# Gates of two more units from sums of logarithms, one unit's keys and queries turned on VectorE, and a load queue in written order

## The chip, the cores and the metric

The kernel runs on one core of a Trainium2 chip. That core has TensorE (PE, with its weight loads shown as PEld), VectorE (DVE), ScalarE (ACT), GpSimd (POOL), a queue engine (SP) that issues nearly all transfers here, and 16 DMA engines. The metric is device microseconds of one execution. The kernel before took 466.81 us in the median of four runs (466.21 to 467.61). A profile records one execution with the start and duration of each instruction; its times are us from the start of its span.

## The reference

There are two blocks, one after the other. The first is a gated linear attention over 4 batches, 8 heads, 768 steps and a head of 48:

```
f = 1 / (1 + exp(-f_logit))
for t in range(S):
    state = f[:, :, t, :, None] * state + k[:, :, t] (outer) v[:, :, t]
    y[:, :, t] = q[:, :, t] @ state
```

The second is a mixer on x, which is y with the heads side by side (768 x 384 per batch):

```
u   = x + ((x^T U) V)^T          # U: 768 x 32, V: 32 x 768
out = u + relu(u @ w_ch1) @ w_ch2   # w_ch1: 384 x 1536, w_ch2: 1536 x 384
```

Inputs are float32, but the four weights arrive as float64, and the kernel rounds them to float32 itself.

## The kernel before

**Units.** The recurrence is done two heads at a time. A unit n is a pair of heads of a batch, so there are 16 (NU); four (HP) make a batch. A unit's 768 steps stand in 12 chunks of 64. Inside a chunk the kernel needs, for each step, the product of the gates after it in the chunk (X, which scales the keys) and the product up to it (Y, in effect one over the first, which scales the queries). With these a chunk is ordinary products: scores of keys and queries (sc, L967), a mask (A, L980), the scores times v (inner, L1077), a turned copy of the keys (kept, L994), the chunk's addition to the state (ds, L1018), a scan over the chunks (L1043) and queries times states (y, L1059).

**Two ways to X and Y.** Units 0 to 3 go by logarithms: `logs` and `logs_end` take log(1 + exp(-f)) on the loaded tile (a floor on VectorE, Exp and Ln on ScalarE), `log_sums` (L820) makes the sums on TensorE by a product with a triangular matrix `later`, which turns the tile as well, and `keep_logs` (L832) takes exponentials of the sums on ScalarE. Units from 4 on go by gates: `gates` (L851) turns f and applies Sigmoid, `keep` (L866) runs a backward scan on VectorE for X with four small instructions after it, and `read` (L884) a forward scan for Y. The tiles `fz` hold the gates and need a zero at each chunk's start (L1269, L1270).

**Three ways to turn.** Channels have to lie in the partitions. For units 0 to 5 `load` (L630) brings the tensors in rows of 48 numbers and TensorE turns them, six 128x128 transposes a tensor (`on_tensor`, L777). Units 6 and later (TURNED is 6) are loaded in blocks of 32 steps in eight smaller transfers for two tensors (L661), and VectorE turns them in 32x32 blocks (`turned`, L754). `operand` (L786) turns keys or queries and multiplies them by X or Y.

**Weights.** 27 blocks of float64: one of U, two of V, twelve of w1, twelve of w2. A block is loaded into a ring of four buffers, halved on ScalarE (two instructions, L91 and L92), joined on VectorE (L98 to L100) and added on POOL (L101). `ahead_by` starts block i+11 when it joins block i; the load has to wait until the block four before it has left its buffer.

**The order around the change.** VectorE and ScalarE run in the order in which the code is written up to the second batch's mixer, TensorE throughout. SP's order is the written one up to `written.close()` (L1246), before mixer 0 starts; behind it a scheduler sets it. The mixer's first product for batch 0 (ch1, L300) then runs as 17 pieces of 12 matmuls, `m.firsts[1:]`, behind one piece that turns x. After each piece a weight block or two is joined, and from piece number EARLY on one step of the generator `second` is taken. `second` first brings the front of unit 4 and then `steps` (L1118) for units 4 to 8, with the fronts of 5 to 9 in between. A front is five pieces: gates, keep, keys, read, queries. `follow` (L768) loads the tensor of two units ahead when a tensor has been used. What is left of `second` after ch1 goes on in `attention`, where `Fill` spreads the pieces of ch2 (L355, three matmul pairs each) evenly over the remaining steps: a fixed number of portions sets the share of each step, and what is left over runs at the end. In before 35 steps and 35 portions remain. The stretch ends with the first product of the next mixer (ph, L184).

PSUM has three large buffers (`big`: transposes, scores, states, y) and two smaller ones (`mm`: ch1 and ch2), used in turn.

Of the kernel before, what the change touches and what calls it, by code (L numbers as in the profile page):

```python
# [14 lines left out]
AF = mybir.ActivationFunctionType  # L15
ALU = mybir.AluOpType
# [11 lines left out]
FLOOR = -40.0  # L28
# [128 lines left out]
class Mixer:  # L157
# [6 lines left out]
    def __init__(self, tc, b, x, U, V, w1, w2, sums, ident, blocks, out, two, three, zp, ps_big, ps_mm, wide=False,  # L164
                 z_all=None, room=None, pair=0):
        nc = tc.nc
# [8 lines left out]
        uT, z, h, S = {}, {}, {}, {}  # L175
# [161 lines left out]
        self.some = low_rank_of, added_up_of, mix_of, turn_of, ch1_of  # L337

        def store(t, o, cols=slice(0, DM)):
            n = 1 if b else 2  # L340
            for r in range(n):
                g = slice(r * P // n, (r + 1) * P // n)
                nc.sync.dma_start(out=out[b, t * P + g.start : t * P + g.stop, cols], in_=o[g, cols])
# [221 lines left out]
def factored_path(ctx, tc, q, k, v, f_logit, moe_U, moe_V, moe_w_ch1, moe_w_ch2, out, ok):  # L565
# [4 lines left out]
    nc = tc.nc  # L570
    B, H, S, D = q.shape
    P = nc.NUM_PARTITIONS
    C = P // 2
# [3 lines left out]
    HP = H // 2  # L577
# [11 lines left out]
    TURNED = HP + HP // 2  # L589
# [40 lines left out]
    def load(n, *names):  # L630

        b, hp = divmod(n, HP)
        for nm in names:
            if nm == "v":
                v_tiles[n] = three.tile([P, NBL, 2, D], F32, name="v_nat")
            for par in range(2):
                head = src[nm][b, 2 * hp + par]
                if nm in "kq" and n < HP:
                    if par == 0:
                        nc.sync.dma_start(  # L640
                            out=packed(n, nm).rearrange("p (h t) -> p h t", h=2),
                            in_=src[nm][b, 2 * hp : 2 * hp + 2].rearrange("h (p c) d -> p h (c d)", p=P),
                        )
                    continue
                if nm == "v" and par:

                    for s in range(2):
                        nc.sync.dma_start(
                            out=v_tiles[n][(1 - s) * C : (2 - s) * C, :, par, :],
                            in_=head.rearrange("(c s p) d -> s p c d", s=2, p=C)[s],  # L650
                        )
                    continue
                if nm == "v" or n < TURNED:
                    dst = v_tiles[n] if nm == "v" else nat[n % 2][nm]
                    nc.sync.dma_start(out=dst[:, :, par, 0:D], in_=head.rearrange("(c p) d -> p c d", p=P))
                    continue
                head = head.rearrange("(c i) d -> i c d", i=NB)
                for part in range(2):
                    p0 = par * PAD + part * NB
                    n_ch = min(NB, D - part * NB)  # L660
                    nc.sync.dma_start(  # L661
                        out=raw[n % 2][nm][p0 : p0 + NB, :].rearrange("p (c d) -> p c d", d=NB)[:, :, 0:n_ch],
                        in_=head[:, :, part * NB : part * NB + n_ch],
                    )
# [95 lines left out]
    def prepare(n):  # L760


        T = units[n] = {}
# [4 lines left out]
        def follow(nm):  # L768

            if n >= HP and n + 2 < NU:  # L770
                load(n + 2, nm)

        def on_tensor(nm):

            pt = ps_big.tile([P, 2, 512], F32, name="pt", tag="big")
            for c in range(NBL):
                nc.tensor.transpose(  # L777
                    pt[:, 2 * c // NBL, c % (NBL // 2) * P : (c % (NBL // 2) + 1) * P],
                    nat[n % 2][nm][:, c].rearrange("p h d -> p (h d)"), ident,
                )  # L780
            return pt[:, :, 0 : G * C].rearrange("p a (c t) -> p a c t", t=C)

        def halves(t):
            return t[:, 0:S].rearrange("p (a c t) -> p a c t", a=2, t=C)

        def operand(nm, of):  # L786
            t = T[nm] = kz[n % 2][:, C:] if nm == "k" else two.tile([P, S], F32, name="qT")
            if n < HP:
                pt = on_tensor(nm).rearrange("p a c t -> p a (c t)").rearrange("p a (c t) -> p t a c", c=NBL // 2)
                by_time = "p (t a c) -> p t a c"  # L790
                nc.vector.tensor_tensor(t.rearrange(by_time, a=2, c=NBL // 2), pt,
                                        T[of].rearrange(by_time, a=2, c=NBL // 2), ALU.mult)
            elif n < TURNED:
                nc.vector.tensor_tensor(halves(t), on_tensor(nm), halves(T[of]), ALU.mult)
            else:
                turned(t, r[nm])
                nc.vector.tensor_tensor(t, t, T[of], ALU.mult)

        def unpack(nm):
            nc.vector.tensor_copy(  # L800
                nat[n % 2][nm][:, :, :, 0:D], packed(n, nm).rearrange("p (h c d) -> p c h d", h=2, c=NBL),
            )
# [47 lines left out]

        def gates():  # L851
            f0 = T["f0"] = two.tile([P, NCH], F32, name="f0")
            if n < TURNED:
                pt = on_tensor("f")
                nc.scalar.activation(halves(f)[:, :, :, 1:C], pt[:, :, :, 1:C], AF.Sigmoid)
                nc.scalar.activation(f0.rearrange("p (a c) -> p a c", a=2), pt[:, :, :, 0], AF.Sigmoid)
                follow("f")
                return
            fT = late[:, 6, :]
            turned(fT, r["f"])  # L860
            follow("f")
            fv = fT.rearrange("p (c t) -> p c t", t=C)
            nc.scalar.activation(by_chunk[:, :, 1:C], fv[:, :, 1:C], AF.Sigmoid)  # L863
            nc.scalar.activation(f0, fv[:, :, 0], AF.Sigmoid)
# [23 lines left out]
        def queries():  # L888
            operand("q", "Y")
            follow("q")  # L890

        if n < HP:
            return [logs, keep_logs, keys, log_sums, queries, logs_end, lambda: unpack("k"), lambda: unpack("q")]
        return [gates, keep, keys, read, queries]

    x_tiles = {}
# [196 lines left out]
    def front(n, *names):  # L1093

        if n >= NU:
            return []
        if n not in ahead:
            names_of = ("gates", "keep", "keys", "read_back", "queries", "gates_end", "unpack_k", "unpack_q")
            ahead[n] = dict(zip(names_of, prepare(n)))
        return [ahead[n].pop(nm) for nm in names if nm in ahead[n]]  # L1100
# [9 lines left out]
    def joined(*groups):  # L1110

        groups = [g for g in groups if g]
        for _ in groups[1:]:
            yield lambda: None
        if groups:
            yield lambda: [f() for g in groups for f in g]

    def steps(first, last):  # L1118

        def behind(n):  # L1120

            return HP + 3 <= n < NU - 1

        for n in range(first, last):
            if n < NU:
                yield from joined(rear(n - 2, "inner"), rear(n - 1, "scores"), rear(n, "kept"))
            else:
                for piece in rear(n - 2, "inner") + rear(n - 1, "scores"):
                    yield lambda: None
                    yield piece  # L1130
            if behind(n):
                yield from front(n, "read_back", "queries")
            if n + 1 < NU and n + 1 not in v_tiles:
                load(n + 1, "v")
            yield from front(n + 1, "gates", "keep", "keys")
            yield from joined(rear(n - 1, "read"), rear(n, "states", "scan"))
            if not behind(n + 1):
                yield from front(n + 1, "read_back", "queries")
            if n + 1 == last:
                yield from rear(n - 1, "inner")  # L1140
                if n + 2 < NU:
                    load(n + 2, "v")
# [30 lines left out]
    with tc.manual_schedule(engines={nc.vector.engine, nc.scalar.engine}):  # L1173
# [66 lines left out]
        low_rank_of, added_up_of, mix_of, turn_of, ch1_of = m.some  # L1240
        for load_w in weights[early + FIRST : early + FIRST + 4]:
            load_w[0]()
        load(HP + 1, "f", "k")
        weights[early + FIRST + 4][0]()
        load(HP + 1, "q", "v")
        written.close()  # L1246
        loads[early]()
        low_rank_of(done)
        for piece in rear(n, "read"):
# [15 lines left out]
        m.before[4][1]()  # L1265
        ch1_of(0, 0, (0, 2), (1, 2))
        loads = loads[early + 3 :]
        for t in fz:
            nc.vector.memset(t[:, 0:S].rearrange("p (c t) -> p c t", t=C)[:, :, 0], 0.0)  # L1269
            nc.vector.memset(t[:, S : S + 1], 0.0)  # L1270

        start = m.before[5:]

        EARLY = 3
        second = chain(front(HP, "gates", "keep", "keys", "read_back", "queries"), steps(HP, 2 * HP + 1))
        for i, (_, piece) in enumerate(start + m.firsts[1:]):
            piece()
            for f in loads[: 2 if i in (0, 2) else 1]:
                loads.remove(f)
                f()  # L1280
            if i >= EARLY:
                next(second)()
        for f in loads:
            f()
        n = len(m.seconds) // (NBL // 2)
        todo, after = m.seconds[:-n], m.seconds[-n:]

# [397 lines left out]
```

## Time and profile before

| what | value |
|---|---|
| median of four runs | 466.81 us |
| the profiled execution's own time | 466.64 us |
| its span, first to last instruction | 464.9 us |
| granted TensorE clock | 0.999 |
| busy: TensorE, VectorE, ScalarE, POOL | 456.1, 352.6, 166.3, 54.4 us |
| ch1 of mixer 0 with units 4 and 5 beside it | 48.15 to 99.40 us |
| ch2 of mixer 0 with units 4 to 7 beside it | 99.40 to 149.48 us |

How to read the lines that follow: a timeline line has the start, the time from the first to the last of its instructions, the engine, the source line, the operation, output and inputs, shapes and count; in brackets stand the idle time of that engine before it and what ended it ("issue" means that the profile shows no cause). A line by stretches has the stretch, its length, then the busy time and count of PE, PEld, DVE, ACT and POOL, the granted clock, the mean share of the DMA engines and GB/s. A float32 matmul is issued as two instructions, a transpose as one. Matmuls overlap, so their spacing, not their duration, is what one costs.

### The profile page before, as it was taken

How to read it: one execution, taken by the hardware profiler on the slowest of the kernel's cores; microseconds unless marked ns; L12 is line 12 of the kernel's file. 1: busy time of each engine (PE TensorE's matmuls, PEld its weight loads, DVE VectorE, ACT ScalarE, POOL GpSimd, SP SyncE). 2: the span in 40 equal slices, each digit the busy share in tenths (PEclk: the TensorE clock that was granted, in tenths of full speed). 3: DMA queues.
4: the chain of work that ended last, by engine and by line, in shares of the span. 5: the costliest groups of instructions: out<-in, count | busy, mean ns of one | idle time of the engine just before them, and what ended most of it. 6: DMA issues, size and time to landing. Idle time of an engine off the chain costs nothing.

```text
span 464.9 us, 13023 instructions
## 1 busy us (share of the span) xinstructions
PE 456.1 (98%) x5639; PEld 395.2 (85%) x5639; DVE 352.6 (76%) x582; ACT 166.3 (36%) x319; POOL 54.4 (12%) x60
## 2 busy tenths in 40 slices
PE   8999999999999999999999999999999999999997
PEld 6886888876666578999898888889989999999996
DVE  5768788979999677676765559977797886858652
ACT  6775776563332143323322222431312311212200
POOL 2002445634112001010000000120000000000000
PEclk9999999999999999999999999999999999999999
DMA  9948997577778704504533030100000000000001
GB/s 194 198 123 208 218 215 184 144 127 106 123 103 123 113 18 53 78 1 89 76 52 76 12 61 4 27 4 21 18 1 1 35 1 19 17 1 35 1 36 39
DMA packets 148583, 34.35 MB, mean 74 GB/s; under 512 B 136934, under 2 KB 146982, under 8 KB 148518
## 3 DMA queue, kind: packets, MB, share of 16 engines
q1 hardware_dynamic: 147718, 33.29, 36.7%
q8 instruction: 46, 0.75, 0.7%
q10 hardware_dynamic: 800, 0.15, 0.2%
q14 instruction: 19, 0.16, 0.1%
HBM read 28.70 MB, written 4.72 MB: 72 GB/s over the span
## 4 chain that ended last, share of the span: by engine, by line
PE 76%; DVE 14%; issue 3%; ACT 3%; DMA 2%; SPq 2%; POOL 0%; DVEq 0%; ACTq 0%; POOLq 0%
PE pw L389 26%; PE pz L300 18%; PE pp L495 12%; PE po L355 5%; PE y L1059 2%; SPq L661 2%; PE pt L777 2%; PE y L1077 1%; PE ds L1018 1%; PE pt L827 1%; PE sc L967 1%; DVE late L868 1%; DVE late L886 1%; PE pt L994 1%; DVE late L921 1%
## 5 line engine op out<-in xcount | busy, mean ns | idle before, releaser
L300 PE MATMUL pz<-uT,w 128*128 128x256 f32 x492 | 111.5, 382 | 0.3 <-ACT uT L289 0.2
L300 PEld LDWEIGHTS pz<-uT,w 128*128 128x128 f32 x492 | 91.7, 190 | 12.9 <-ACT uT L289 0.6
L1047 POOL COPY st<-added 128x576 f32<-128x576 f32 x12 | 18.2, 1519 | 187.5 <-DVE added L1043 187.5
L389 PE MATMUL pw<-zw,w_raw 128*128 128x192 f32 x216 | 38.0, 329 | 0.0
L389 PE MATMUL pw<-w,z_all 128*128 128x192 f32 x216 | 37.3, 327 | 0.0
L101 POOL TENSOR_TENSOR w<-w_y,w_r 128x384 int32<-128x384 int32 x24 | 31.5, 1314 | 36.9 <-DVE w_y L100 20.7
L389 PEld LDWEIGHTS pw<-w,z_all 128*128 128x128 f32 x216 | 35.3, 190 | 0.5
L389 PEld LDWEIGHTS pw<-zw,w_raw 128*128 128x128 f32 x216 | 35.1, 190 | 0.6 <-DVE w_y L204 0.3
L335 ACT ACTIVATE z_all<-pz 128x512 f32<-128x512 f32 x33 | 19.6, 598 | 44.3 <-PE pz L300 43.9
L868 DVE TENSOR_TENSOR_SCAN late<-fz,late 128x768 f32<-128x768 f32 x12 | 21.1, 1755 | 9.4 <-ACT fz L863 9.3
L488 ACT ACTIVATE other<-other 128x512 f32<-128x512 f32 x18 | 11.3, 632 | 40.3 <-DVE other L204 40.3
L355 PE MATMUL po<-w,zw 128*128 128x384 f32 x72 | 25.1, 495 | 0.0
L355 PE MATMUL po<-w,z_all 128*128 128x384 f32 x72 | 24.7, 493 | 0.0
L886 DVE TENSOR_TENSOR_SCAN late<-fz,other 128x768 f32<-128x768 f32 x12 | 22.0, 1835 | 0.2
L980 DVE TENSOR_TENSOR A<-sc,causal 128x768 f32<-128x768 f32 x16 | 15.2, 952 | 8.7 <-PE sc L967 8.7
L355 PEld LDWEIGHTS po<-w,zw 128*128 128x128 f32 x72 | 13.2, 190 | 9.6 <-issue 0.8
L355 PEld LDWEIGHTS po<-w,z_all 128*128 128x128 f32 x72 | 13.3, 190 | 8.9 <-DVE o L204 0.6
L488 ACT ACTIVATE z_all<-z_all 128x512 f32<-128x512 f32 x12 | 7.6, 631 | 34.1 <-DVE z_all L204 34.1
L1026 ACT COPY added<-ds 48x576 f32<-48x576 f32 (+2 forms) x29 | 17.9, 620 | 5.1 <-PE ds L1018 4.7
L1059 PEld LDWEIGHTS y<-st,qT 48*64 48x64 f32 x704 | 13.6, 137 | 6.6 <-issue 4.3
L495 PE MATMUL pp<-v_nat,late 128*128 128x128 f32 x152 | 19.1, 275 | 0.0
L98 DVE TENSOR_SCALAR w_y<-w_y 128x384 f32<-128x384 f32 (+3 forms) x27 | 12.2, 451 | 8.8 <-ACT w_y L91 8.6
(226 smaller groups left out, 869.0 us busy)
## 6 DMA issues: line engine op xcount, KB each, us to landing
w_raw<-in_moe_w_ch_dram SPq DMA_DIRECT2D x18, 384.0 KB, 3.6
out_dram<-o SPq DMA_DIRECT2D x17, 192.0 KB, 1.9
v_nat<-in_v_dram SPq DMA_DIRECT2D x16, 144.0 KB, 3.6
v_nat<-in_v_dram SPq DMA_DIRECT2D x32, 72.0 KB, 3.5
zw<-in_moe_w_ch_dram SPq DMA_DIRECT2D x6, 384.0 KB, 5.0
out_dram<-o SPq DMA_DIRECT2D x14, 96.0 KB, 2.2
w<-in_k_dram SPq DMA_DIRECT2D x4, 288.0 KB, 4.0
w<-in_q_dram SPq DMA_DIRECT2D x4, 288.0 KB, 4.4
```

The source lines that it names most:

```text
L101: nc.gpsimd.tensor_tensor(dst.bitcast(I32), shaped(y.bitcast(I32)), shaped(r), ALU.add)
L300: nc.tensor.matmul(pm[:, i * 2 * P : (i + 1) * 2 * P], lhsT=w1[:, m, o : o + P], rhs=uT[a][:, m, :], start=(m == 0), stop=(m == NDC - 1))
L335: nc.scalar.activation(z[a, c][:, k : k + 2, :].rearrange("p i t -> p (i t)"), pm, AF.Relu)
L355: nc.tensor.matmul(pm, lhsT=z[a, i // NI][:, i % NI, s * P : (s + 1) * P], rhs=w2[:, i, :], start=(i == 0), stop=(i == NFC - 1))
L389: nc.tensor.matmul(W["pm"][:, n * HM : (n + 1) * HM], lhsT=lhs[:, i, :], rhs=rhs[:, i, :], start=(i == 0), stop=(i == NI - 1))
L488: nc.scalar.activation(dst, dst, AF.Relu, scale=float(SIGNS[n]))
L495: nc.tensor.matmul(pm[:, i, r * P : (r + 1) * P], lhsT=room["w"](wn)[:, r * P : (r + 1) * P], rhs=x_node(a, xn), start=((xn, wn) == of[0]) ...
L868: nc.vector.tensor_tensor_scan(backwards(X, S - 1, S), backwards(f, S, S), backwards(ends, S - 1, S), 0.0, ALU.mult, ALU.add,)
L886: nc.vector.tensor_tensor_scan(Y, f[:, 0:S], starts, 0.0, ALU.mult, ALU.add)
L1026: nc.scalar.copy(added[r, 1:].rearrange("p (e c s) -> p e c s", c=NBL, s=2)[:, e], ds[r, :, 0 : NBL * D].rearrange("p s (c e) -> p e c s", ...
L1047: nc.gpsimd.tensor_copy(st, states.rearrange(by_e, c=NCH))
L1059: nc.tensor.matmul(o(c % 2, par, c // 2), lhsT=T["q"][rows[par], chunk[c]], rhs=T["st"][rows[par], c, :], start=(c <= 2), stop=False, skip ...
```

## The change

1. `load`: units up to 4 come in rows for all tensors, unit 5 for f alone. Keys and queries of unit 5 come in blocks of 32 and VectorE turns them.
2. Units 4 and 5 get new pieces in place of gates, keep and read: `bound` (the floor on VectorE), `sums_kept` (sums on TensorE, the load of the next f, the exponentials on ScalarE) and `logs_whole` (Exp and Ln on ScalarE). Their scans, sigmoids and small VectorE instructions are gone. The table of Sigmoid is first loaded by unit 6. The zeros of `fz` are written by units 6 and 7.
3. Order: `bound` and `logs_whole` of unit 4 stand ahead of `second`, those of unit 5 are joined to keys and queries of unit 4. EARLY becomes 4. So 48 steps remain in `second` instead of 50, 34 are left after ch1, and `Fill` counts 36 portions.
4. SP keeps the written order to the end of ch1; the keys and queries of unit 5 are loaded behind pieces 0 and 2.
5. `store` writes the last four blocks of batch 0 in one transfer each instead of two.

```diff
         def store(t, o, cols=slice(0, DM)):
-            n = 1 if b else 2
+            n = 2 if b == 0 and t < 2 else 1
...
-                if nm == "v" or n < TURNED:
+                if nm == "v" or n <= HP or (nm == "f" and n < TURNED):
...
         def gates():
             f0 = T["f0"] = two.tile([P, NCH], F32, name="f0")
-            if n < TURNED:
-                pt = on_tensor("f")
-                nc.scalar.activation(halves(f)[:, :, :, 1:C], pt[:, :, :, 1:C], AF.Sigmoid)
-                nc.scalar.activation(f0.rearrange("p (a c) -> p a c", a=2), pt[:, :, :, 0], AF.Sigmoid)
-                follow("f")
-                return
+            if n < TURNED + 2:
+                nc.vector.memset(by_chunk[:, :, 0], 0.0)
+                nc.vector.memset(f[:, S : S + 1], 0.0)
...
+        def bound():
+            fn = nat[n % 2]["f"][:, :, :, 0:D]
+            nc.vector.tensor_single_scalar(fn, fn, FLOOR, ALU.max)
+
+        def logs_whole():
+            fn = nat[n % 2]["f"][:, :, :, 0:D]
+            nc.scalar.activation(fn, fn, AF.Exp, scale=-1.0)
+            logs_end()
+
+        def sums_kept():
+            log_sums()
+            follow("f")
+            keep_logs()
+
         if n < HP:
             return [logs, keep_logs, keys, log_sums, queries, logs_end, lambda: unpack("k"), lambda: unpack("q")]
+        if n < TURNED:
+            return [bound, sums_kept, keys, logs_whole, queries]
         return [gates, keep, keys, read, queries]
...
-        load(HP + 1, "f", "k")
+        load(HP + 1, "f")
         weights[early + FIRST + 4][0]()
-        load(HP + 1, "q", "v")
-        written.close()
+        load(HP + 1, "v")
...
-        for t in fz:
-            nc.vector.memset(t[:, 0:S].rearrange("p (c t) -> p c t", t=C)[:, :, 0], 0.0)
-            nc.vector.memset(t[:, S : S + 1], 0.0)
-
         start = m.before[5:]
 
-        EARLY = 3
-        second = chain(front(HP, "gates", "keep", "keys", "read_back", "queries"), steps(HP, 2 * HP + 1))
+        EARLY = 4
+        second = chain(front(HP, "keep"), joined(front(HP, "keys"), front(HP + 1, "gates")),
+                       joined(front(HP, "queries"), front(HP + 1, "read_back")), steps(HP, 2 * HP + 1))
+        bound, logs = front(HP, "gates", "read_back")
+        bound()
         for i, (_, piece) in enumerate(start + m.firsts[1:]):
             piece()
+            if i == 1:
+                logs()
+            elif i in (0, 2):
+                load(HP + 1, "k" if i == 0 else "q")
             for f in loads[: 2 if i in (0, 2) else 1]:
                 loads.remove(f)
                 f()
             if i >= EARLY:
                 next(second)()
         for f in loads:
             f()
+        written.close()
```

More of the change, by code (lines that the diff above doesn't have):

```diff
@@ L781, in on_tensor @@
             return pt[:, :, 0 : G * C].rearrange("p a (c t) -> p a c t", t=C)
-        def halves(t):
-            return t[:, 0:S].rearrange("p (a c t) -> p a c t", a=2, t=C)
         def operand(nm, of):
@@ L792, in operand @@
                                         T[of].rearrange(by_time, a=2, c=NBL // 2), ALU.mult)
-            elif n < TURNED:
-                nc.vector.tensor_tensor(halves(t), on_tensor(nm), halves(T[of]), ALU.mult)
+            elif n == HP:
+                nc.vector.tensor_tensor(
+                    *[u.rearrange("p (a c t) -> p a c t", a=2, t=C) if u is not None else on_tensor(nm) for u in (t, None, T[of])],
+                    ALU.mult,
+                )
             else:
```

## The prediction

> **What bounds the kernel now.** I read the page's first two parts first, then the table by stretches, then the timelines of TensorE and VectorE in the stretch that the diff touches. The page, its busy times (engine, busy us, share of the span):
>
> ```profile
> PE 456.1 (98%) x5639; PEld 395.2 (85%) x5639; DVE 352.6 (76%) x582; ACT 166.3 (36%) x319; POOL 54.4 (12%) x60
> ```
>
> TensorE is busy for 456.1 of 464.9 us, so all its idle time is 8.8 us; 3.4 lie after its last product. The granted clock is 0.999, so no time hides there. The table by stretches (length, busy us and counts of PE, PEld, DVE, ACT, POOL, clock, DMA share, GB/s), cut where the mixer's ch1 (L300) ends and ch2 (L355) begins:
>
> ```profile
> 48.15:99.40 51.25, 51.25 (x364) 44.59 (x361) 45.90 (x75) 34.48 (x67) 26.28 (x21) 1.00 0.81 186
> 99.40:150.59 51.19, 50.41 (x866) 32.06 (x864) 45.37 (x61) 18.15 (x35) 10.67 (x7) 1.00 0.78 113
> ```
>
> In the first stretch TensorE never stops: work taken from other engines there is worth nothing, only TensorE's own instructions count. In the second it stops a little, and VectorE is nearly as full. The stops, in TensorE's timeline (start, us, count, idle time before):
>
> ```profile
> 99.40 4.03 PE L355 MATMUL po<-w,z_all 128*128 128x384 f32 x12
> ...
> 104.73 4.41 PE L355 MATMUL po<-w,zw 128*128 128x384 f32 x12
> ...
> 116.69 0.76 PE L1018 MATMUL ds<-v_nat,kb 64*48 64x48 f32 x48 [0.57 <-issue]
> ...
> 123.00 0.59 PE L994 MATMUL pt<-ident,kz 64*128 64x64 f32 x12
> ...
> 134.88 0.59 PE L994 MATMUL pt<-ident,kz 64*128 64x64 f32 x12 [0.21 <-DVE kz L797]
> ```
>
> Twelve po products take 3.97 us where they run freely (99.40 to 103.36); at 104.73 they take 4.35 (to 109.08): 0.38 of waiting for the last w2 block, whose POOL sum ends at 108.18. At 116.69 ds of unit 6 needs the PSUM buffer that the mask A of unit 5 frees; y before it needs 0.71 us elsewhere (103.36 to 104.07), so this stop is 116.69 - 115.22 - 0.71 = 0.76. The third is 0.21. Together 1.35 us. VectorE's timeline shows who is late:
>
> ```profile
> 101.94 0.97 DVE L754 STREAM_TRANSPOSE late<-late 128x768 f32<-128x768 f32 x1
> ...
> 105.65 1.75 DVE L868 TENSOR_TENSOR_SCAN late<-fz,late 128x768 f32<-128x768 f32 x1
> ...
> 109.52 0.96 DVE L797 TENSOR_TENSOR kz<-kz,late 128x768 f32<-128x768 f32 x1
> ...
> 115.64 0.95 DVE L980 TENSOR_TENSOR A<-sc,causal 128x768 f32<-128x768 f32 x1
> 116.51 0.97 DVE L754 STREAM_TRANSPOSE late<-other 128x768 f32<-128x768 f32 x1
> 118.37 1.76 DVE L868 TENSOR_TENSOR_SCAN late<-fz,late 128x768 f32<-128x768 f32 x1 [0.90 <-ACT fz L863]
> ...
> 121.65 0.96 DVE L797 TENSOR_TENSOR kz<-kz,late 128x768 f32<-128x768 f32 x1
> ```
>
> kz of unit 6 starts at 109.52, of unit 7 at 121.65: one unit costs VectorE 12.13 us, with 0.90 of waiting for the sigmoid. Here VectorE sets the pace of the keys and TensorE can only follow.
>
> **The change, part by part: TensorE.** Out go the gates' transposes of units 4 and 5 and the keys' and queries' of unit 5: 4 x 6 (L777), each six 0.66 us (56.02 to 56.68), 2.62. In come the sums of logarithms, 2 x 12 instructions of 130 columns (L827). Their row is 12 in 1.53 us (26.41 to 27.94). From below: the L300 rows give 256 columns in 216 ns (24 in 5.18), by the column 110 ns for 130, 1.32 per unit. I take 1.54, the same line's own row: +3.08. Net +0.46, from below +0.02, all of it in the full first stretch.
>
> **VectorE, first stretch.** Out: per unit scan, copies and reciprocal 2.85 (63.37 to 66.22) and the second scan 1.67 (69.83 to 71.50), 9.0 for two. In: two bounds (0.45, row L808) and two turnings of unit 5 (0.97, row L754), 2.9. Some 6 us of relief, worth nothing: VectorE has 5.35 us of idle time there already and waits for the weights' ACT halves, which TensorE's pieces pace.
>
> **ScalarE, first stretch.** In: Exp and Ln (0.69 each, L810 and L817) and the kept exponentials (0.8, 0.8, 0.2, 0.2), 3.4 per unit; out two sigmoids of 0.76 and a table load of 1.28. That adds 4.0 us to 34.48 of 51.25: hidden by the rest of 16.8. If the cover failed, ch1's PSUM buffers would come free late; each has a 2.6 us piece between filling and need, and the longest delay that I add up (Exp and Ln, 1.4) is under it. Memsets (0.07 each) have cover.
>
> **Loads.** The SP queue keeps to its written order. Keys of unit 5 stand behind weight block 16, queries behind 19, f of unit 6 behind 23, k behind 25. A weight load waits for the block four before it; by the rows of before (block 19's space free at 76, f's at 84.4, k's at 90.9) f6 is issued by 87 and k6 by 94, landing 3 to 4 us later. They are needed at some 100 and 108. v of unit 6 has similar room. The finer loads split each 192-byte row in two (32 and 16 numbers), 3,072 packets more; q1's 35,584 packets between 45 and 110 us take 80.6% of 16 engines, 23.6 ns each, so 4.5 us of all engines. Slack covers that: nothing. Four stores less leave SP about 2 us that no one waits for.
>
> **Where it turns: VectorE's order after ch1.** One piece more runs before unit 4 starts (EARLY 4), but unit 4 and 5 have two pieces fewer, so the gates of unit 6 come one ch1 piece earlier, after the last but one. Count from that piece's end (T); w(24) to w(26) are the last of the 27 weight blocks. By before's spacings: evacuation T+0.20, ACT's block w(24) 0.69, VectorE's w(24) 1.27, turning of f6 at 2.6, sigmoid at 3.6 (1.00 after, 101.94 to 102.94). The new queue: the last piece's evacuation and w(25) now stand behind this sigmoid on ACT (free at 4.46), and on VectorE w(25) stands ahead of the scan. So w(25) starts at 5.53, the scan at 6.80, and w(26) is now behind the scan: 9.65 (2.86 after it, as 105.65 to 108.51). Turning of k6 at 10.93, kz at 11.94, against 12.71 in before (109.52 - 96.81): only 0.77 earlier. kz of unit 7 starts 12.13 later at 24.07 and ends at 25.03; with the 0.12 to its reader, kept of unit 7 can't start before T+25.15.
>
> TensorE gets there earlier, since fewer ch2 products stand in front: ch1's last piece 2.6, three po 2.0, y and ds 1.4, nine po 6.0 (with a wait for w(26), ready at about 12.1 and wanted at 11.3, up to 0.9), inner, scores and kept 2.1, six po 4.0, y and ds 1.4, three po 2.0, inner and scores 1.6: 23.1 to 24.2. It waits 1 to 2 us. In before kept of unit 7 starts at 123.00, T+26.19, with one piece of ch2 more done (2.03). So after is 25.15 + 2.03 - 26.19 = 0.99 behind; the 0.21 of unit 8 falls away, since nine po now stand before it: +0.78. From below: with no wait at all -1.35. From above: two of the blocks' L99 at 1.05 instead of 0.36, as where POOL runs beside, +1.4 more: +2.2. I take +0.78, by the rows of the same instructions. Later the same work follows in the same order and TensorE stays full, so nothing gives it back.
>
> **Sum.** +0.46 + 0.78 = +1.24 us on the profiled execution's 466.64 (span 464.9 and 1.74 around it): 467.88. The median, 466.81, is 0.17 above that execution, so 468.05; I say 468.0.
>
> **Rules weighed.** Row: the table load takes 1.28 and the sigmoid starts 0.01 after it (58.97, 60.26). The Trainium skill, "ScalarE: Activation LUTs", "What ACT_TABLE_LOAD costs", counts a further drain, 2.66 us in all. The load moves to the sigmoid of unit 6, between w(24) on ACT and T+3.6, where 1.28 fits; by the page the sigmoid and all behind it would be 0.7 us later, 468.8 as an estimate. The row decides. A second page speaks against the turnings: "VectorE: DVE Perf Modes", "Rules for kernel authors", gives 128x128 transposes to TensorE where PSUM will do; here the rows are 0.97 on VectorE against 0.66 on the engine that has no idle time.
>
> **Rivals.** (a) VectorE isn't late: the relief carries over, kz of unit 7 is there when TensorE comes. For it: only 0.77 us of waiting separates VectorE's blocks at T. Against it: every block waits for an ACT half paced by TensorE. It decides when kz of unit 7 is 1.9 us earlier than I work out; then +0.46 - 1.35 = -0.89, with the cheap sums -1.33: 465.5 to 465.9. (b) Half of it: kz of unit 7 some 0.5 to 1.2 earlier (no long copy, 0.17 instead of 0.78 at L873): 466.9 to 467.5, no change. (c) The written queue holds a load back: a weight block late by one piece (2.6) delays f6, then k6 and v6. For it: DMA share 0.81. Against it: 5 us or more of slack. 469 to 471. (d) The change doesn't do what it says, for one a second table load: 1.28 once more on ACT; the built order of ACT holds one, so I give it nothing.
>
> **How the numbers follow.** Forecast 0.5 (467.5 to 468.7), (a) 0.17, (b) 0.22, (c) 0.11. Two tenths of a per cent, 0.93 us, is about what runs of this kernel tell apart (466.21 to 467.61). Slower is most of the forecast and (c), without the forecast's lower end: 0.52; no change (b) and that end, and a part of (a): 0.33; faster the rest of (a): 0.15. The range takes in half of (a) and the lower half of (c): 465.8 to 469.6.
>
> **What would show it.** Right: 48 new L827 rows less 24 of the L777 kind and no idle time of TensorE in ch1; kz of unit 7 ending about 25 us after ch1's last but one piece, and an idle time of 0.5 us or more before L994's like of unit 7 with kz as releaser; w(26) after the scan on VectorE; the stop before ds of unit 6 gone. Wrong: no idle time before that kept, or sums of 12 in 1.3 us, or a wait for a DMA in ch1.

## The result, and the profile after

The changed kernel takes 468.07 us in the median of 47 runs (467.05 to 474.12). The kernel before, in 74 runs beside it and later, takes 467.25 us, 0.44 more than in its first four. The ratio is 1.0015, with a 95% interval of 1.0008 to 1.0021: 0.7 us slower (0.4 to 1.0), real, but under the 0.93 us that the prediction took as the bound of no change.

The profiled execution of the changed kernel took 468.04 us, its span is 466.2, the granted clock 0.999. Its busy times by engine:

```profile
PE 455.4 (98%) x5639; PEld 394.9 (85%) x5639; DVE 345.4 (74%) x574; ACT 169.7 (36%) x327; POOL 47.7 (10%) x60
```

VectorE does 7.2 us less, POOL 6.7 less, ScalarE 3.4 more, and TensorE has as many instructions as before and 0.7 us less that counts as busy, although the span is longer. By stretches (start and end, length, then busy us and count of PE, PEld, DVE, ACT and POOL, clock, DMA share, GB/s), cut where ch1 starts, where the first ch2 product starts and where the next mixer's ph starts:

```profile
48.62:99.91 51.29, 51.29 (x364) 44.83 (x361) 37.78 (x68) 37.80 (x75) 20.56 (x20) 1.00 0.78 180
99.91:150.69 50.78, 49.06 (x849) 31.50 (x847) 44.64 (x64) 18.22 (x36) 10.47 (x7) 1.00 0.82 119
```

The first stretch of the kernel before is shown above (51.25 long); the second, cut at ph as here:

```profile
99.40:149.48 50.08, 49.30 (x849) 31.64 (x848) 44.26 (x60) 18.15 (x35) 9.56 (x7) 1.00 0.78 113
```

ch1 is 0.04 longer, the stretch behind it 0.70. That makes 0.74, the size of the measured ratio. The rest of what separates these two executions can't be put down to the change: ch1 starts 0.47 later (48.62 against 48.15), and what follows ph is 0.09 longer (315.51 against 315.42). Ahead of ch1 the two differ only on VectorE, which has four memsets of 0.07 us or less fewer and the floor of unit 4 (0.45) more; and in the eight executions with the changed kernel's code up to there ch1 starts anywhere from 47.65 to 49.62 (47.65 to 50.03 in all 14 profiled for this study). The lengths of the two stretches, however, repeat to 0.1 us where nothing in them was changed and the granted clock stayed full. So the experiments are read by stretches first and by medians second.

The stops of TensorE behind ch1, from its timeline (start, us, operation; in brackets the idle time before and what ended it):

```profile
105.35 3.39 PE L355 MATMUL po<-w,zw 128*128 128x384 f32 x10
109.51 0.91 PE L355 MATMUL po<-w,zw 128*128 128x384 f32 x2 [0.77 <-POOL w L101]
...
120.74 0.89 PE L980 MATMUL sc<-qT,kz 48*64 48x64 f32 x48
122.58 0.59 PE L1007 MATMUL pt<-ident,kz 64*128 64x64 f32 x12 [0.95 <-DVE kz L797]
```

The first is the wait for w(26), whose POOL sum now stands behind the scan; the second is the wait of unit 7's kept for its keys. The stop before ds of unit 6 is gone. VectorE in the same time:

```profile
98.59 0.36 DVE L98 TENSOR_SCALAR w_y<-w_y 128x384 f32<-128x384 f32 x1 [0.67 <-ACT w_y L91]
...
99.89 0.97 DVE L754 STREAM_TRANSPOSE late<-late 128x768 f32<-128x768 f32 x1
...
102.81 0.36 DVE L98 TENSOR_SCALAR w_y<-w_y 128x384 f32<-128x384 f32 x1 [1.95 <-ACT w_y L91]
...
104.12 1.75 DVE L865 TENSOR_TENSOR_SCAN late<-fz,late 128x768 f32<-128x768 f32 x1
...
106.97 0.35 DVE L98 TENSOR_SCALAR w_y<-w_y 128x384 f32<-128x384 f32 x1
...
109.24 1.03 DVE L797 TENSOR_TENSOR kz<-kz,late 128x768 f32<-128x768 f32 x1
...
121.47 0.96 DVE L797 TENSOR_TENSOR kz<-kz,late 128x768 f32<-128x768 f32 x1
```

This is the queue that the prediction wrote down: turning of f6, w(25), scan, w(26), keys. The 1.95 us before w(25) is VectorE waiting for ScalarE, which does the sigmoid and the evacuation first. Keys of unit 6 start at 109.24, those of unit 7 12.23 later.

### The profile page after: what moved, and what is told of

It reads as the page before. It is cut to its first block, busy times and chain, and to the rows that moved or that the text cites. A ratio compares the mean times of both kernels' runs of the same rounds, so it can differ in the third digit from the quotient of the medians.

```text
span 466.2 us, 13028 instructions
## 1 busy us (share of the span) xinstructions
PE 455.4 (98%) x5639; PEld 394.9 (85%) x5639; DVE 345.4 (74%) x574; ACT 169.7 (36%) x327; POOL 47.7 (10%) x60
## 4 chain that ended last, share of the span: by engine, by line
PE 80%; DVE 9%; SPq 4%; issue 3%; DMA 2%; ACT 2%; POOL 0%; DVEq 0%; POOLq 0%
PE pw L389 25%; PE pz L300 20%; PE pp L495 12%; PE po L355 7%; SPq L661 3%; PE y L1072 2%; PE y L1090 2%; PE sc L980 2%; PE ds L1031 2%; PE pt L827 2%; PE pt L1007 1%; PE pt L777 1%; DVE late L934 1%; PE put L288 1%; DMA w<-in_q_dram 1%
## 5 line engine op out<-in xcount | busy, mean ns | idle before, releaser
L300 PE MATMUL pz<-uT,w 128*128 128x256 f32 x492 | 111.2, 382 | 0.3
L300 PEld LDWEIGHTS pz<-uT,w 128*128 128x128 f32 x492 | 91.9, 190 | 13.0 <-ACT uT L289 0.6
L1060 POOL COPY st<-added 128x576 f32<-128x576 f32 x12 | 16.9, 1405 | 188.8 <-DVE added L1056 188.8
L101 POOL TENSOR_TENSOR w<-w_y,w_r 128x384 int32<-128x384 int32 x24 | 26.3, 1095 | 43.0 <-DVE w_y L100 29.4
L98 DVE TENSOR_SCALAR w_y<-w_y 128x384 f32<-128x384 f32 (+3 forms) x27 | 10.1, 375 | 16.2 <-ACT w_y L91 16.2
L865 DVE TENSOR_TENSOR_SCAN late<-fz,late 128x768 f32<-128x768 f32 x10 | 17.6, 1756 | 5.4 <-ACT fz L860 5.2
L883 DVE TENSOR_TENSOR_SCAN late<-fz,other 128x768 f32<-128x768 f32 x10 | 19.4, 1938 | 0.2
```

The source lines that it names most:

```text
L101: nc.gpsimd.tensor_tensor(dst.bitcast(I32), shaped(y.bitcast(I32)), shaped(r), ALU.add)
L300: nc.tensor.matmul(pm[:, i * 2 * P : (i + 1) * 2 * P], lhsT=w1[:, m, o : o + P], rhs=uT[a][:, m, :], start=(m == 0), stop=(m == NDC - 1))
L865: nc.vector.tensor_tensor_scan(backwards(X, S - 1, S), backwards(f, S, S), backwards(ends, S - 1, S), 0.0, ALU.mult, ALU.add,)
L883: nc.vector.tensor_tensor_scan(Y, f[:, 0:S], starts, 0.0, ALU.mult, ALU.add)
L1060: nc.gpsimd.tensor_copy(st, states.rearrange(by_e, c=NCH))
```

## The experiments

Theory V is the prediction's: in ch1 only TensorE's own instructions count, and behind ch1 VectorE paces the keys of units 6 to 8. All lengths below are ch1 and the stretch behind it, in the order "ch1 / behind", from each kernel's profiled execution; before has 51.25 / 50.08, the changed kernel 51.29 / 50.78. Medians of before in the three series of runs were 467.14, 467.14 and 467.40.

**Fewer portions.** `Fill` gives the remaining steps more ch2 pieces each, so one more stands ahead of unit 7's kept.

```diff
-        attention(second, Fill(todo, 10 + 10 * HP - (len(start) + len(m.firsts) - 1 - EARLY)))
+        attention(second, Fill(todo, 8 + 10 * HP - (len(start) + len(m.firsts) - 1 - EARLY)))
```

> The changed kernel with ch2's pieces spread over 34 portions, the number of steps that are left, instead of 36. Eight pieces of ch2 then stand before the turned keys (kept) of unit 7 instead of seven. Theory V (VectorE is late with the keys of unit 7 and TensorE has too little other work): the 0.95 us of waiting before kept of unit 7 goes, nothing else moves: 0.95 us faster than the changed kernel, 467.1 us beside 467.25 for the kernel before, ratio 0.9995. Theory S (the loss sits in the first stretch or earlier, and the waits behind it only take another place): no gain, 468.0, ratio 1.0015.

Measured: 466.66 us, ratio 1.0000 (0.9976 to 1.0025); 51.29 / 49.76. The interval of the ratio alone doesn't set this version apart from the changed kernel; the stretch does, and the three later versions with 34 portions repeat it (49.72 to 50.00). TensorE's timeline in this run:

```profile
108.53 0.91 PE L355 MATMUL po<-w,zw 128*128 128x384 f32 x2 [0.76 <-POOL w L101]
...
116.89 4.14 PE L355 MATMUL po<-w,zw 128*128 128x384 f32 x12
...
122.52 0.59 PE L1007 MATMUL pt<-ident,kz 64*128 64x64 f32 x12
```

Twelve products stand between y and inner of unit 5, ahead of unit 7's kept, where the changed kernel has six (a piece of ch2 is six), and the stop of 0.95 is gone; the stretch is 1.02 shorter. The waiting was the cost of work in the wrong place, as V has it, and not of work added.

**w(26) ahead of unit 6's keys.**

```diff
-            for f in loads[: 2 if i in (0, 2) else 1]:
+            for f in loads[: 2 if i in (0, 2, len(m.firsts) - 1) else 1]:
```

> The changed kernel with the last weight block joined right after the last but one, ahead of the scan of unit 6 on VectorE. Theory V: TensorE's 0.77 us of waiting for that block goes, but the keys of unit 6 and 7 come no earlier, and up to 0.7 us later, since the second join then runs beside POOL's sum (L99 1.05 us instead of 0.36); the wait before kept of unit 7 grows from 0.95 to between 1.7 and 2.4 us: 468.0 to 468.8, ratio 1.0015 to 1.003. Theory W (the wait for the weight block is itself the loss): 0.77 us faster than the changed kernel, 467.3, ratio 1.0000.

Measured: 469.45 us, 1.0044 (1.0022 to 1.0067); 51.30 / 51.39. TensorE's wait for w(26) is gone, but:

```profile
117.16 0.76 PE L1031 MATMUL ds<-v_nat,kb 64*48 64x48 f32 x48 [0.57 <-issue]
123.26 0.59 PE L1007 MATMUL pt<-ident,kz 64*128 64x64 f32 x12 [1.65 <-DVE kz L797]
```

VectorE does the block before the scan, its second instruction takes 1.04 instead of 0.36, keys of unit 6 start 0.7 later (10.02 behind ch1's end against 9.33), and what TensorE gained it waits for at unit 7. V stands. That the median is above the expectation goes with a lower clock in six of the ten runs, told in the last section.

**Both together.**

> The changed kernel with Fill's portions 34 and w(26) joined before unit 6's keys, together. By the theory (VectorE paces the keys behind ch1): TensorE's wait for w(26), 0.77, goes, but kz of unit 7 comes some 0.8 later and meets a slack of about 1.1 that the extra ch2 piece gives, so some 0.5 of waiting comes back: 466.4 to 467.0 us, ratio 0.9985 to 1.0000, no better than 34 portions alone by more than 0.3. By the rival, that the place of w(26) costs VectorE nothing: 0.76 less than with 34 portions alone, 465.9, ratio 0.997.

Measured: 467.16 us, 0.9997 (0.9982 to 1.0011); 51.30 / 50.00, with stops of 0.57 at ds of unit 6 and 0.25 at kept of unit 8. No better than the portions alone: the place of w(26) is not free on VectorE.

**EARLY back to 3.** Every step of `second` comes one ch1 piece earlier; 33 steps are then left after ch1, and `Fill` counts 35 portions.

```diff
-        EARLY = 4
+        EARLY = 3
```

> The changed kernel with EARLY 3 as in the kernel before: every step of units 4 to 8 comes one piece of ch1 earlier, so that the keys of unit 6 are turned within the last piece of ch1, some 3.5 us after its end instead of 9.3. Theory V: both waits of TensorE behind ch1 (0.77 for the last weight block, 0.95 for the keys of unit 7) go: 1.7 us faster than the changed kernel, 466.3, ratio 0.998. Theory S: no gain, 468.0, ratio 1.0015. If a load comes late for the earlier steps (the tensors of unit 6), an idle time of TensorE or VectorE with a transfer as its cause appears in the last pieces of ch1, and 1 to 3 us are lost.

Measured: 468.33 us, 1.0013 (0.9989 to 1.0037); 51.31 / 51.11. A miss: I had expected a gain. VectorE in this run:

```profile
98.31 0.97 DVE L754 STREAM_TRANSPOSE late<-late 128x768 f32<-128x768 f32 x1
...
101.22 0.36 DVE L98 TENSOR_SCALAR w_y<-w_y 128x384 f32<-128x384 f32 x1 [1.94 <-ACT w_y L91]
...
107.60 1.03 DVE L797 TENSOR_TENSOR kz<-kz,late 128x768 f32<-128x768 f32 x1
108.55 0.35 DVE L98 TENSOR_SCALAR w_y<-w_y 128x384 f32<-128x384 f32 x1
...
111.06 2.49 DVE L883 TENSOR_TENSOR_SCAN late<-fz,other 128x768 f32<-128x768 f32 x1
```

Keys of unit 6 do come 2.7 earlier, counted from ch1's end (6.67 behind it against 9.33). But the same wait for ScalarE's halves is there, one more weight block then stands between these keys and unit 7's, the scan takes 2.49 beside POOL instead of 1.73, and the keys of unit 7 start 20.91 behind ch1's end against 21.56. Two thirds of a microsecond is left, and TensorE, which reaches units 6 to 8 with fewer ch2 products ahead, waits 0.71, 0.18 and 0.91. I had moved the work and not its waits.

**Unit 5's turning back on TensorE.**

```diff
-                if nm == "v" or n <= HP or (nm == "f" and n < TURNED):
+                if nm == "v" or n < TURNED:
...
-            elif n == HP:
+            elif n < TURNED:
```

> The changed kernel with the keys and queries of unit 5 loaded in rows and turned on TensorE again, 12 transposes of 109 ns in the stretch in which TensorE never stops. If only TensorE's own instructions count in that stretch: 1.3 us slower than the changed kernel, 469.4, ratio 1.0043; VectorE's two turnings less (1.9 us) buy nothing. If VectorE's work counts there: the same or faster, 467 to 468.1.

Measured: 469.52 us, 1.0041 (1.0020 to 1.0063); 52.61 / 50.72. ch1 is 1.32 longer: twelve transposes by 109 ns, 1.31. The stretch behind it does not notice.

**The turning alone, on the kernel before.**

> The kernel before with one part of the change alone: keys and queries of unit 5 come in blocks of 32 and VectorE turns them (12 transposes less on TensorE, two turnings of 0.97 us more on VectorE). By the theory that in the first stretch only TensorE's own instructions count: 12 x 109 ns = 1.31 us less in ch1 of mixer 0, the stretch behind it unchanged, so 467.25 - 1.31 = 465.9 us, ratio 0.997. By the rival, that VectorE's load in this stretch counts as well: 1.94 us more on VectorE would delay the evacuations of ch1, and the time would stay at 467.2 or above, with idle time of TensorE between the pieces of L300.

Measured: 468.92 us, 1.0042 (1.0026 to 1.0058); 49.94 / 52.60. ch1 is 1.31 shorter, to the hundredth as expected, and yet the kernel is slower. (In this execution the clock falls behind the stop, see the last section; the next experiment has 52.20 at full clock.) My theory of ch1 held and my reading of what stands behind it did not. TensorE, then VectorE:

```profile
103.48 3.49 PE L355 MATMUL po<-w,zw 128*128 128x384 f32 x10
109.13 0.91 PE L355 MATMUL po<-w,zw 128*128 128x384 f32 x2 [2.15 <-POOL w L101]
```

```profile
84.33 0.97 DVE L754 STREAM_TRANSPOSE kz<-other 128x768 f32<-128x768 f32 x1
85.33 1.02 DVE L797 TENSOR_TENSOR kz<-kz,late 128x768 f32<-128x768 f32 x1
...
95.35 0.97 DVE L754 STREAM_TRANSPOSE qT<-other 128x768 f32<-128x768 f32 x1
...
106.54 1.75 DVE L868 TENSOR_TENSOR_SCAN late<-fz,late 128x768 f32<-128x768 f32 x1
...
110.41 0.96 DVE L797 TENSOR_TENSOR kz<-kz,late 128x768 f32<-128x768 f32 x1
```

VectorE has no idle time from 78.83 to 103.8 here. The two turnings push the last weight blocks and the keys of unit 6 by 0.9 (110.41 against 109.52), TensorE arrives 1.3 earlier, and it waits 2.15 for w(26).

**The same, with the loads where the change has them.** The rival to that reading was the queue: in the run above the finer loads stand ahead of weight block 10. Here they stand behind pieces 0 and 2, and the written order reaches to the end of ch1.

```diff
-        load(HP + 1, "f", "k")
+        load(HP + 1, "f")
...
-        load(HP + 1, "q", "v")
-        written.close()
+        load(HP + 1, "v")
...
             piece()
+            if i in (0, 2):
+                load(HP + 1, "k" if i == 0 else "q")
...
+        written.close()
```

> The kernel before, with keys and queries of unit 5 turned on VectorE as in the run of that part alone, but their loads stand behind pieces 0 and 2 of ch1 and SP's written order reaches to the end of ch1, as in the change. That run lost 2.36 us behind ch1 by a late w(26). By the theory that VectorE, which stands full from 80 to 103 us there, delays the last blocks by the 1.94 us of the turnings: nothing changes, 468.9 us, ratio 1.004, again some 2 us of waiting for w(26). By the rival, that the finer loads ahead of weight block 10 delay the blocks: the wait falls back to 0.4 and the 1.1 to 1.3 us of ch1 stay gained: 466.0, ratio 0.9975.

Measured: 468.60 us, 1.0025 (1.0005 to 1.0046); 49.94 / 52.20, with the same wait for w(26):

```profile
109.33 0.91 PE L355 MATMUL po<-w,zw 128*128 128x384 f32 x2 [2.14 <-POOL w L101]
```

The place of the loads in the queue is out of it; the lateness is VectorE's. Counted from ch1's start, ph comes 102.14 us later against 101.33 in before, 0.81 more, and so much later do the keys of unit 6 come (62.18 against 61.37): in this run the end moves with VectorE's keys, and the 1.31 that TensorE saved is lost in waiting.

**All three tensors of unit 5 turned, on the kernel before** (`TURNED = HP + 1`).

> The kernel before with f, keys and queries of unit 5 all turned on VectorE (18 transposes less on TensorE, three turnings more on VectorE). By the theory: 1.97 us less in ch1 of mixer 0, nothing behind it: 465.3 us, ratio 0.996. By the rival (VectorE counts): no gain over the version with keys and queries alone, or a loss.

Measured: 473.53 us, 1.0142 (1.0124 to 1.0160); 50.27 / 54.12 in the profiled run, the fastest of four (470.63). A stop of 0.75 for an evacuation now falls within ch1, and the wait for w(26) is 3.39. More work on an engine that has no room loses more; in the median a lower clock has a part too (0.981 to 0.996 in the four runs).

**VectorE's relief given back, early and late.** The changed kernel with six VectorE products of zeros by zeros more (they change no value), behind pieces 5 to 10, or behind pieces 12 to 17:

```diff
             piece()
+            if 5 <= i <= 10:
+                nc.vector.tensor_tensor(starts, starts, starts, ALU.mult)
```

> The changed kernel with six VectorE products of 0.95 us on the tile of zeros more, one behind each of pieces 5 to 10 of ch1: 5.7 us of VectorE's relief given back in the first stretch. By the theory that VectorE's time there is worth nothing: 468.1 us as the changed kernel, ratio 1.0015 within 0.002, and the same length from L300's start to ch1's end (51.3 us). By the rival, that VectorE's relief in this stretch was needed to hold the loss to 0.7: 1 to 5 us slower, 469 to 473.

> The changed kernel with six VectorE products of 0.95 us more behind pieces 12 to 17 of ch1, where the run before had them behind 5 to 10 and lost nothing in ch1 or behind it. By the theory that VectorE paces the keys of units 6 and 7 from the last weight blocks on: the products behind the last two or three pieces delay them in full, the earlier ones in part: 2 to 5 us slower than the changed kernel, 470 to 473, ratio 1.007 to 1.013. By the rival, that VectorE has room throughout ch1: 468.1 to 468.5.

Measured: early 468.37 us, 1.0032 (1.0014 to 1.0050), 51.30 / 50.73, keys of unit 6 9.27 behind ch1's end against 9.33; late 475.51 us, 1.0166 (1.0142 to 1.0190), 51.29 / 58.07. The two kernels by stretches, early first:

```profile
49.04:100.34 51.30, 51.30 (x365) 44.84 (x361) 45.80 (x75) 37.84 (x75) 22.92 (x20) 1.00 0.79 181
100.34:151.07 50.73, 49.06 (x849) 31.49 (x847) 44.63 (x64) 18.20 (x36) 10.47 (x7) 1.00 0.82 118
```

```profile
49.21:100.50 51.29, 51.29 (x364) 44.83 (x361) 38.82 (x65) 36.53 (x73) 20.82 (x19) 1.00 0.72 170
100.50:158.57 58.07, 53.53 (x849) 34.00 (x848) 49.83 (x71) 20.01 (x38) 11.49 (x8) 0.91 0.76 113
```

8 us more on VectorE in the early part (37.78 to 45.80: the products, and some weight-block instructions that take longer between them, L98 1.15 instead of 0.36) move neither stretch; the early median is 0.3 above the changed kernel's, within the two intervals. The same six instructions near the end of ch1 cost 7.3 us, more than their own 5.7, and more than I had expected. Not all of that is VectorE's time: the keys of unit 6 come 4.0 later (13.37 behind ch1's end), TensorE waits 2.66 and 1.88 for weight blocks, and then it runs at half clock from some 113 to 123 us, which the mean of 0.91 shows. So the same busy time is free or dear by its place: what counts is whether it stands ahead of the last weight blocks and unit 6's front with no gap left to take it up.

**A version from these findings.** The changed kernel has VectorE busy for 5.41 of 10 us from 70 to 80 and 6.97 from 80 to 90, so it has room for two more turnings: unit 4's keys and queries too, with 34 portions. Once with unit 4's loads at their place, once with these loads behind the f of unit 5.

```diff
-                if nm == "v" or n <= HP or (nm == "f" and n < TURNED):
+                if nm == "v" or n < HP or (nm == "f" and n < TURNED):
...
-            elif n == HP:
-                nc.vector.tensor_tensor(
-                    *[u.rearrange("p (a c t) -> p a c t", a=2, t=C) if u is not None else on_tensor(nm) for u in (t, None, T[of])],
-                    ALU.mult,
-                )
...
-        attention(second, Fill(todo, 10 + 10 * HP - (len(start) + len(m.firsts) - 1 - EARLY)))
+        attention(second, Fill(todo, 8 + 10 * HP - (len(start) + len(m.firsts) - 1 - EARLY)))
```

> The same with unit 4's keys and queries loaded at their old place, ahead of the weight blocks of ch1. By the theory 465.4 us as well if the transfers had room there. DMA engines were at 0.98 and more before ch1 in the kernel before, and ch1's start moved with them, so I expect ch1 to start 0.5 to 1.5 us later than in the version with later loads: 466 to 467, ratio 0.998 to 1.0.

> The changed kernel with 34 portions, and unit 4's keys and queries turned on VectorE too (12 transposes less on TensorE), their finer loads moved behind the f of unit 5. In the first stretch VectorE was busy there for 0.54 to 0.74 of the time from 70 to 90 us, so two turnings (1.94 us) have room: ch1 1.31 us shorter, the stretch behind it as with 34 portions alone (49.8): 466.66 - 1.3 = 465.4 us, ratio 0.997. By the rival, that the queue holds the finer loads or the weight blocks behind them back: TensorE idle within ch1 for a DMA or a late block, 467 or above.

Measured: loads at their place 465.97 us, 0.9974 (0.9964 to 0.9985), 49.99 / 49.72; loads later 466.45 us, 0.9999 (0.9972 to 1.0025), 49.99 / 49.75. The first by stretches:

```profile
47.97:97.96 49.99, 49.99 (x352) 43.63 (x349) 40.71 (x70) 37.73 (x75) 20.58 (x20) 1.00 0.85 192
97.96:147.68 49.72, 49.01 (x850) 31.48 (x848) 44.42 (x64) 18.41 (x36) 10.40 (x7) 1.00 0.80 116
```

ch1 is 1.30 shorter in both, as worked out, and nothing is lost behind it. The version with the loads at their place is 1.2 us faster than the kernel before and, by the two ratios, which come from different series of runs, some 1.9 us faster than the changed one, the best of this study. My preference for later loads was wrong or at least not borne out: in that profiled run ch1 starts at 50.03 and the times scatter from 464.99 to 471.38. A part of the late start is the clock's: it is at 0.50 from 40 to 42 us there, ahead of ch1, and at full in the profiled run of the other version, which starts ch1 at 47.97. Whether the later loads have a share, or this is the scatter of the start seen in all kernels, was not settled.

## Why the prediction was right, and where it was off

**The time.** 468.0 was forecast and 468.07 measured, but that nearness is luck; two errors cancel in it: the forecast loss of 1.24 us was half a microsecond too large, and the base, the median of four runs, was 0.44 below what 74 runs gave. The ratio, 1.0015, lies almost wholly within "no change" as the text drew it, to which it gave 0.33, less than the 0.52 for slower.

**TensorE in ch1, +0.46.** The mechanism held, since ch1 has no stop in any run of the changed kernel's order and its length follows TensorE's instructions to 0.02 us (portions, EARLY, products of zeros: 51.29 to 51.31; twelve transposes more: 52.61; twelve fewer: 49.99). The size failed at "I take 1.54, the same line's own row". In ch1 the sums of a unit take 1.34:

```profile
59.08 1.50 PE L827 MATMUL pt<-later,late 128*128 128x130 f32 x12
60.42 1.89 PE L300 MATMUL pz<-uT,w 128*128 128x256 f32 x8
...
77.99 1.50 PE L827 MATMUL pt<-later,other 128*128 128x130 f32 x12
79.33 1.89 PE L300 MATMUL pz<-uT,w 128*128 128x256 f32 x8
```

From start to next start 1.34 both times, so 2 x 1.34 - 2.62 = +0.06; measured +0.04. The prediction had named sums of "12 in 1.3 us" as a sign of being wrong, and for this term it was. The bound from below, by the column from the L300 rows, was the better row: it came from the same stretch, where TensorE is full, and the row I took came from the early one. Why the sums take 1.53 there (26.41 to 27.94) was not looked into. The prediction's own sign of being right counts "48 new L827 rows" for 24 of L777; it is 24 for 24 (48 to 72, and 84 to 60).

**Behind ch1, +0.78.** Measured +0.70. Counted from the end of the last but one piece (99.91 less a piece's 2.59, 97.32), the keys of unit 6 start at 11.92 (forecast 11.94), unit 7's 12.23 later (12.13), kept of unit 7 at 25.26 (25.15). The two waits are 0.77 (up to 0.9) and 0.95 (1 to 2). Kept is thus 1.10 behind, where 0.99 was worked out, and 0.40 comes back after it, where only the 0.21 of unit 8 was counted. The portions show the step: one ch2 piece more ahead of kept, and the loss is gone.

**ScalarE, nothing.** Right: no evacuation is late in ch1. The table load has its room:

```profile
99.03 1.28 ACT L860 ACT_TABLE_LOAD   x1
100.90 0.83 ACT L860 ACTIVATE fz<-late 128x756 f32<-128x756 f32 x1 [0.58 <-DVE late L754]
```

The sigmoid's releaser is VectorE's turning. By the 2.66 us of the Trainium skill, "ScalarE: Activation LUTs", "What ACT_TABLE_LOAD costs", it could not have started before 101.69; it starts at 100.90, so here the row of 1.28 decides.

**Loads, nothing.** Right: f6 was issued at 85.02 (forecast by 87) and k6 at 92.41 (by 94), and no stop of TensorE has a transfer as its releaser. That rival (c) didn't come about is shown for these loads at this place only.

**VectorE's relief, "worth nothing".** True of the net, wrong as a reading of the stretch. (The relief is larger than the 6 us worked out: 45.90 to 37.78.) The text held 5.35 us of idle time in ch1 against two turnings. But that idle time lies early; from 80 us VectorE is full in the kernel before, and there the turnings alone lose more than they gain (the two runs above with the turning on the kernel before: +1.2 and +0.8 by the stretches). With the logarithms in place the same turning gains its 1.31 and loses nothing (the run with the turning back on TensorE): the scans that they take away pay for it. So the change is one trade, and the parts can't be costed one by one (the logarithms were not run without EARLY 4 and the 36 portions): the logarithms cost TensorE 2 x (1.34 - 0.66) = 1.36 and free VectorE, and the turning uses a part of that room to take 1.31 back. What is left over of the relief, the early part, is worth nothing, as the products of zeros show.

**Rivals.** (a) and (b), the relief carrying over to unit 7, fell: its keys came 0.1 later than worked out, not 0.5 to 1.9 earlier. The four stores less were not tried alone; what follows ph differs by 0.09 between the two executions.

## What to carry to other kernels

Busy time and idle time of a whole stretch don't say what an instruction costs an engine that is off the critical path: look from its place to the next instruction that another engine waits for, and whether any idle time lies between. Take a duration from a row in the stretch where the instruction will stand, not from the same line elsewhere. When work is moved in front of a fixed sequence, the filler that covered its waits has to be spread anew: here two portions of one constant were worth more, by the stretches, than the whole change lost (1.02 against 0.74).

## What the runs showed of the hardware

A short idle time of TensorE can cost more than itself. In the turning-alone run the 2.15 us stop was followed by a lower granted clock (window, its length, busy us and counts, clock after POOL):

```profile
107.00:109.00 2.00, 0.00 (x0) 0.00 (x0) 1.97 (x2) 0.00 (x0) 2.00 (x1) 1.00 0.91 132
109.00:111.00 2.00, 1.87 (x46) 1.33 (x50) 1.93 (x6) 0.00 (x0) 0.07 (x1) 0.80 0.83 148
111.00:112.00 1.00, 1.00 (x48) 1.00 (x45) 1.00 (x2) 0.60 (x1) 0.00 (x0) 0.50 1.03 130
112.00:113.00 1.00, 1.00 (x34) 0.88 (x30) 1.00 (x2) 0.04 (x1) 0.23 (x1) 0.50 0.19 24
113.00:114.00 1.00, 1.00 (x12) 0.75 (x9) 1.00 (x1) 0.41 (x1) 1.00 (x1) 0.69 0.64 68
```

Half clock for some 3.4 us, and 48 inner products took 1.39 instead of 0.92. The run with the later loads had a stop of 2.14 and kept a clock of 1.00, so such a stop is followed by it sometimes and not always. It shows in the times: of ten runs with w(26) early (stop 1.65 in the profiled one), the four at a mean clock of 1.00 took 467.8 to 468.6 us, as expected, and the six at 0.996 took 469.3 to 471.2; of twelve runs with later loads, the six at 1.00 took 467.6 to 468.6 and the six at 0.995 to 0.996 took 468.6 to 469.6. With the 2.66 and 1.88 us stops of the late products of zeros, all five were at 0.991 or lower, which fits their cost above 5.7 us. In all, 25 of 37 runs of the five kernels whose profile shows a stop of 1.65 us or more behind ch1 had a mean clock below 0.998, and 29 of 216 of the other kernels, among them the 86 runs of before in the three series. The stops of 0.77 and 0.95 us of the changed kernel left the clock of their windows at 1.00. But a long stop isn't needed: in the profiled run of unit 4's turning with later loads the clock fell ahead of ch1, again to half for some 3.4 us (0.77, 0.50, 0.50, 0.52 in the four windows from 39 to 43), and the stops just before were 0.47 and 0.69. Where it fell in runs without a profile is not on record. The Trainium skill, "TensorE: Matmul & The Clock Gate", "What's actually happening", has the gate close after an idle window of about 3.4 us in a free-running count; the half clock and its length agree, the stops of 2.15, 0.69 and 0.47 us are shorter than that, and why it fell after them was not tried.

VectorE and POOL take longer where they work side by side: POOL's sum of a weight block takes 1.00 alone and 2.32 beside a scan, and VectorE's L99 0.36 alone and 1.04 beside such a sum. POOL's 60 instructions took 54.4 us in the kernel before and 47.7 in the changed one, which has four scans less.
